# Where the first operands of the down product are loaded, in a forward and backward kernel on one core

## The chip, the cores and the metric

The kernel runs on one core of a Trainium2 chip. The metric is device time in microseconds (us), the median of several executions; lower is better. The core's engines that matter here are TensorE (PE, matrix products), VectorE (DVE, elementwise work), ScalarE (ACT, mostly copies out of PSUM), and the queues on which transfers (DMAs) are issued: SyncE's (SP), ScalarE's and GpSimd's (POOL). Each engine and each queue takes its instructions in the order in which the compiled program holds them.

## The reference

The reference is the vector-Jacobian product of one layer, with its forward output. Only these lines bear on the change:

```python
xn = _layernorm(x, axis=-1)                  # x: 2048 x 1024
s  = _A_ref(xn, A_k, A_v, ...)               # a long convolution, by Fourier transforms
g  = einsum("bsd,df->bsf", xn, w_gate)       # F = 3584
u  = einsum("bsd,df->bsf", xn, w_up)
h  = g * u
bm = einsum("bsf,fd->bsd", h, w_down)        # the down product
out = x + s * silu(bm)
# outputs: out and the gradients of all inputs and weights
```

## The kernel before, in words

All matrices are bf16 in 128-row blocks. The part around the change is the forward pass; it takes about the first 570 us of the span.

**The gate/up stage** (line 645) makes g and u. The weights come in 14 slabs of 256 columns of each matrix (`load_slab`, line 536, two transfers of 512 KB, two buffers `wslab`). A unit (`gu_unit`, line 629) takes one slab and four row blocks: 32 matmuls of 512 columns into `psg` (two PSUM buffers), four ACT casts to `gut` (line 647; two SBUF buffers in the last slabs), one store of `gut` to DRAM (`GUd`, line 654, on ACT's queue). The product h = g*u of a unit (`hN`, line 659, on DVE) is traced at the first row of the next unit. The turn of h (`turn`, line 669) comes a unit later still, after the second row of the unit after next: eight transposes on PE (line 674), one ACT copy to `hT` (line 675; two buffers from pool `fg` here), and the store of turned h to DRAM (`store`, line 664; `HTd`, 256 KB, on SP's queue through the helper `ld`, line 60).

**The convolution** runs beside it. Its DVE instructions are fixed in program order among those of the units (`pinned`, line 207, names most DVE lines as L213). `tick()` at the end of each row of a unit lets the generator `conv_forward` go on by an amount from its planned costs.

**The last two slabs**, 12 and 13, are done in eight units, line 951 on: slab 12 on row blocks 0-3 and 4-7, slab 13 on the same, then both again on row blocks 8-15. I number these units u0 to u7, and the units of slab 11 before them u-4 to u-1.

**The down product** (`bm_mm`, line 966, PSUM tiles `psbm`) starts behind u7. For its first two row blocks it reads turned h from `HT0` (two SBUF areas: `HT0[0]` holds h's blocks of 128 features 0 to 15, `HT0[1]` those from 16 on) and the down weight from `WD` (seven pieces of 512 rows, 1 MB each). `load_wd(j)` (line 937) and `ht_rows` (line 940) give their sources. Each of the first 28 feature blocks takes four matmuls: two row blocks by two halves of the output's columns. The areas of `WD` and `HT0` are eight old buffers, `U0` to `U7`, that were free at that point or come free as the last units stop reading their rows.

Program order is not the order in which a queue issues. The planner of the framework orders what is traced by its own estimates, unless something ties it: `tc.issue_after(x)` makes each traced instruction that is on x's engine or queue come behind x in that queue; it adds no semaphore. In the kernel before, line 947 ties `load_wd(0)`, `load_wd(1)` and the load of the whole of `HT0[0]` behind `slab_ld`, the last transfer of slab 13. The load of the first half of `HT0[1]` (line 963) is traced behind u1 and is tied to nothing.

Of the kernel before, what the change touches and what calls it, by code (L numbers as in the profile page):

```python
# [19 lines left out]
def build_kernel(  # L20
# [12 lines left out]
    P = 128  # L33
# [6 lines left out]
    SLW = 256  # L40
    NSL = F // SLW
# [18 lines left out]
    def ld(out, in_):  # L60
        return nc.sync.dma_start(out=out, in_=in_)
# [3 lines left out]
    def st(out, in_):  # L65
        ins = nc.gpsimd.dma_start(out=out, in_=in_)  # L66
        if PINQ[0]:
            tc.keep_in_program_order(ins)
        return ins

    def sta(out, in_):
        return nc.scalar.dma_start(out=out, in_=in_)
# [39 lines left out]
    HTd = [[dram.tile([n, S // 2], BF16, name=f"HTd{i}{n}") for n in (24 * P, 4 * P)] for i in range(2)]  # L112
# [99 lines left out]
    def tt(o, a, b, op):  # L212
        pinned(V.tensor_tensor(o, a, b, op))  # L213
# [35 lines left out]
    def fwd4_half(x, i, wp, psp, first=None):  # L249

        pe_us[0] += 1.75
        SP = wp.tile([P, 2, 2, 512], F32, name="SP", bufs=2)
        for par in range(2):
            ps = psp.tile([P, 2, 2, 256], F32, name="psF")
            cmm(ps[:, 0], T4[par], x, (i, i + 4), first if i == 0 else None, True)
            cmm(ps[:, 1], T4[par], x, (i + 2, i + 6))
            nc.scalar.copy(out=SP[:, :, par], in_=ps[:].rearrange("p s k x -> p s (k x)"))
        return SP

    def fwd4_buf(wp):  # L260
        return wp.tile([P, 2, 2, 4, 256], F32, name="W", tag="W")
# [244 lines left out]
    def u8(i, pat="p (a x) -> p a x", **kw):  # L506
        return U[i][:].rearrange(pat, **kw)
# [94 lines left out]
    def turn_late():  # L602
        for i, (x, q, qi) in enumerate(turn_rows):
            ps = ps_st.tile([P, DC, P], BF16, name="tr")
            for dc in range(DC):
                tr_ln[0] = nc.tensor.transpose(ps[:, dc, :], x[:, dc * P:(dc + 1) * P], ident[:])
            act_copy[0] = nc.scalar.copy(out=XNT[q][:, :, qi * P:(qi + 1) * P], in_=ps[:])
        turn_rows.clear()
# [6 lines left out]
    def defer(fn):  # L615
        later.append([0, fn])

    def flush(age=0):

        for e in later:  # L620
            e[0] += 1
        while later and later[0][0] >= age:
            later.pop(0)[1]()
# [5 lines left out]
    def gu_unit(sl, b0, n, w, tick):  # L629

        if n == 4:
            turn_of[0] += 1
            if turn_of[0] % 3 == 0 and sl < NSL - 2:
                gut = U[5][:, 2048:4096].rearrange("p (a i f) -> p a i f", a=2, i=4)
            else:
                gut = fg.tile([P, 2, 4, SLW], BF16, name="gut")
            hN = fg.tile([P, 2, 4, P], BF16, name="hN", bufs=3)
        else:
            gut = lnp.tile([P, 2, 2, SLW], BF16, name="gut_s", bufs=6)
            hN = lnp.tile([P, 2, 2, P], BF16, name="hN_s", bufs=6)  # L640
        for i in range(n):
            q, qi = divmod(b0 + i, 4)
            ps = ps_gu.tile([P, 512], F32, name="psg")
            for dc in range(DC):
                gu_mm[0] = nc.tensor.matmul(ps[:], XNT[q][:, dc, qi * P:(qi + 1) * P],  # L645
                                            w[:, dc].rearrange("p a f -> p (a f)"), start=(dc == 0), stop=(dc == DC - 1))
            nc.scalar.copy(out=gut[:, :, i], in_=ps[:].rearrange("p (a f) -> p a f", a=2))  # L647
            flush(5)
            if i == 0:
                turn_late()  # L650
            hn[0]()
            hn[0] = nop
            tick()
        sta(GUd[sl, b0 // 8][:, :, b0 % 8:b0 % 8 + n], gut[:, :, 0:n])

        def multiply():
            with tc.issue_after(last.ins) if b0 + n <= 4 and chunk[0] <= 2 else nullcontext():
                by_half = lambda t: t.rearrange("p i (a f) -> p a i f", a=2)
                tt(hN[:, :, 0:n], by_half(gut[:, 0, 0:n]), by_half(gut[:, 1, 0:n]), MUL)
            st(Hd[sl][:, :, b0:b0 + n, :], hN[:, :, 0:n])  # L660
            defer(turn)
        hn[0] = multiply

        def store(hT):
            fr, so = sl % 12 * SLW, b0 % 8 * P
            ld(HTd[b0 // 8][sl // 12][fr:fr + SLW, so:so + n * P].rearrange("(a f) s -> f a s", f=P),
               hT[:, :, 0:n].rearrange("f a i s -> f a (i s)"))

        def turn():
            hT = fg.tile([P, 2, 4, P], BF16, name="hT") if chunk[0] > 5 else lnp.tile([P, 2, 4, P], BF16, name="hT_s", bufs=5)  # L670
            ps = ps_tr.tile([P, 2, 4, P], BF16, name="tr")
            for a in range(2):
                for i in range(n):
                    nc.tensor.transpose(ps[:, a, i, :], hN[:, a, i, :], ident[:])  # L674
            nc.scalar.copy(out=hT[:, :, 0:n], in_=ps[:, :, 0:n])
            store(hT)

    h_out = []
    EIGHT = ((0, 0), (0, 1), (7, 0), (7, 1))
    INV8 = (2, 4, 5, 6, 7)  # L680
    SHIFT_W = 8 * 2.3
# [3 lines left out]
    def conv_forward():  # L685
# [78 lines left out]
        def half(ds, x, i, first=None):  # L764
            if (ds, int(first is not None)) not in EIGHT:
                return fwd4_half(x, i, cf, ps_cv, first)
            SP = cf.tile([P, 2, 2, 512], F32, name="SP", bufs=2)
            fwd8_half(x, i, SP, ps_cv, first, True)
            return SP

        def transform(ds, kind, sp, X, C, ahead, step):

            if ds == 7 and kind == 1:
                S_["forward"] = False
            if (ds, kind) in EIGHT:
                W = fwd4_buf(cs)[:].rearrange("p a b c x -> p (a b c) x")
# [29 lines left out]
        for ds in range(8):  # L806
# [9 lines left out]
            own_room = lambda X: X[:].rearrange("p a x -> p (a x)").bitcast(F32).rearrange("p (a x) -> p a x", a=8)[:, 0:4]  # L816
            eight = (ds, 1) in EIGHT
            if ds == 0:
# [40 lines left out]
    F_TOTAL = 4 * SHIFT_W + 3.0 + 8 * (0.5 + FWD4_W + 1.3 + PROD_W + INV_W) + 10.0 - 0.95 * 8 * (4 * 1.75 + 0.95 + 4 * 0.9)  # L859
    F_TOTAL += len(EIGHT) * (FWD8_W - 9.6 + 0.95 * 1.75) - 2.0  # L860
    F_TOTAL += len(INV8) * (INV8_W - INV_W + 0.95 * 1.8)
# [56 lines left out]
    def tick(by=1):  # L918
        cnt[0] += by
        if cnt[0] == -4:  # L920
            pump((SHIFT_W + 4.05) / F_TOTAL)
        if cnt[0] >= -2:
            pump((SHIFT_W + (F_TOTAL - SHIFT_W) * (cnt[0] + 6.5) / (NT + 3.5)) / F_TOTAL)
# [13 lines left out]
    def load_wd(j):  # L937
        return ld(WD[j], B_w_down[j * 512:(j + 1) * 512, :].rearrange("(c p) d -> p c d", p=P))

    def ht_rows(bp, f0, f1):  # L940
        j = (bp % 4) * 256
        return HTd[bp // 4][f0 // 24][f0 % 24 * P:(f0 % 24 + f1 - f0) * P, j:j + 256].rearrange("(c f) s -> f c s", f=P)
# [3 lines left out]
    HT0 = [u8(4, a=16), u8(5, a=16)]  # L946
    with tc.issue_after(slab_ld.ins):
        load_wd(0)
        load_wd(1)
        ld(HT0[0], ht_rows(0, 0, 16))  # L950
    for hf in range(2):
        if hf == 1:
            load_wd(2)
        for sl in range(NSL - 2, NSL):
            for b0 in (8 * hf, 8 * hf + 4):
                gu_unit(sl, b0, 4, slabs[sl - NSL + 2], tick)
            if (hf, sl) == (1, NSL - 2):
                wd_ld = load_wd(3)
                ld(HT0[1][:, 8:12], ht_rows(0, 24, 28))
            if (hf, sl) == (0, NSL - 2):  # L960

                assert len(h_out) == 8
                ld(HT0[1][:, 0:8], ht_rows(0, 16, 24))
    hn[0]()

    def bm_mm(ps, ht, i, fc):
# [606 lines left out]
def kernel(  # L1573
# [22 lines left out]
    out_9: bass.AP,  # L1596
):
    build_kernel(
        ctx, tc,
        A_q, A_k, A_v, A_shift_k, A_ssm_k, A_ssm_D, B_x, B_w_gate, B_w_up, B_w_down, grad_out,  # L1600
# [32 lines left out]
```

## Time and profile before

| what | value |
|---|---|
| median of three runs | 1928.96 us (1928.41 to 1929.06) |
| the profiled execution, its own time | 1929.12 us |
| its span in the profile | 1927.3 us |
| PE busy in the span | 1910.5 us (99%) |
| DVE busy | 1554.9 us (81%) |
| ACT busy | 638.9 us (33%) |
| units u0 to u7 on PE | about 448.0 to 518.3 us |
| first matmul of the down product | 518.27 us |
| SP queue, loads in question: `HT0[1]` first half, 512 KB | issued 445.85 us |
| slab 13, two of 512 KB | issued 448.22 and 448.65 us |
| `WD[0]`, `WD[1]`, 1 MB each | issued 451.43 and 452.96 us |
| `HT0[0]`, 1 MB | issued 456.75 us |

All times in the text are us from the start of the span. A row of a timeline has the start, the time taken, the engine, the line of the kernel, the operation, output and input tiles, the count that was merged into it, and in brackets the idle time of the engine ahead of it and what ended it. The rows of an engine named SPq or ACTq are transfers being issued; the time taken is that of the issue, and the landing comes later. Buffer numbers are left out: `U<-HTd` is a load of turned h into one of the `U` areas. A row of the table of windows has the stretch, its length, the busy time (and instruction count) of PE, PEld (weight loads), DVE, ACT and POOL, the clock granted to PE as a share of full speed, the busy share of the transfer engines, and GB/s.

### The profile page before, as it was taken

The numbers are of one execution on the slowest core, as the hardware profiler recorded it, in microseconds if no ns is written. First come the engines' busy times: TensorE is split into PE (matmuls) and PEld (weight loads), VectorE is DVE, ScalarE is ACT, GpSimd is POOL, SyncE is SP. The second block draws the span as 40 slices with busy tenths as digits, with TensorE's granted clock in tenths as the row PEclk, the third lists the DMA queues.
The fourth block names the chain that finished last, engine by engine and source line by source line (L and its number), as shares of the span: only waits on it lengthen the run. The fifth ranks groups of instructions, "written<-read, shape, count | busy, mean of one in ns | idle before, by whom it ended". The sixth has DMA issues, their size and how long they took to land.

```text
span 1927.3 us, 27409 instructions
## 1 busy us (share of the span) xinstructions
PE 1910.5 (99%) x10946; PEld 1027.7 (53%) x10946; DVE 1554.9 (81%) x1715; ACT 638.9 (33%) x943; POOL 330.1 (17%) x461
## 2 busy tenths in 40 slices
PE   8999999999999999999999999999999999999999
PEld 5555655554544456665666666664444444444444
DVE  8999999999967555888899999999996403387884
ACT  5754655545422233342222322222222102011113
POOL 5121212201112211000122131021111101011111
PEclk9999999999999999999999999999999999999999
DMA  8786867768789988656778788575797999899884
GB/s 291 270 261 217 260 208 236 222 216 270 253 267 318 307 291 254 210 200 222 261 242 263 236 247 262 202 266 182 225 253 175 140 213 219 162 183 183 196 183 157
DMA packets 451359, 444.41 MB, mean 231 GB/s; under 512 B 268800, under 2 KB 371612, under 8 KB 436768
## 3 DMA queue, kind: packets, MB, share of 16 engines
q1 hardware_dynamic: 394848, 243.36, 47.8%
q0 software_dynamic: 40064, 169.95, 27.8%
q10 hardware_dynamic: 16320, 29.36, 4.2%
q8 instruction: 85, 1.39, 0.3%
q14 instruction: 42, 0.34, 0.1%
HBM read 194.00 MB, written 185.64 MB: 197 GB/s over the span
## 4 chain that ended last, share of the span: by engine, by line
PE 94%; DVE 2%; DMA 2%; ACT 1%; issue 0%; SPq 0%; ACTq 0%
PE psb L1341 20%; PE psx L1471 20%; PE psg L645 18%; PE psb L1324 10%; PE psb L1419 9%; PE psbm L968 9%; PE psF L235 3%; PE psY L438 1%; PE tr L674 1%; DMA HTd<-hT 1%; PE psY L1127 1%; PE psx L1419 1%; DVE W L213 1%; PE psY L449 1%; DVE bst L561 0%; DMA wslab<-in_B_w_gate_dram 0%
## 5 line engine op out<-in xcount | busy, mean ns | idle before, releaser
L645 PE MATMUL psg<-wslab,U 128*128 128x512 bf16 x1792 | 409.5, 380 | 7.3 <-ACT gut L647 4.6
L1341 PE MATMUL psb<-U,U 128*128 128x512 bf16 x1792 | 397.1, 379 | 0.0
L1471 PE MATMUL psx<-U,dgut 128*128 128x512 bf16 x1536 | 332.8, 379 | 0.0
L1471 PEld LDWEIGHTS <-dgut 128*128 128x128 bf16 x1792 | 175.3, 98 | 211.4
L1341 PEld LDWEIGHTS <-U 128*128 128x128 bf16 x1792 | 175.2, 98 | 198.0
L645 PEld LDWEIGHTS <-U 128*128 128x128 bf16 x1792 | 172.9, 98 | 193.4 <-issue 9.0
L1324 PE MATMUL psb<-wdt,U 128*128 128x256 bf16 x1792 | 205.6, 273 | 0.0
L1324 PEld LDWEIGHTS <-U 128*128 128x128 bf16 x1792 | 175.3, 98 | 29.2
L213 DVE TENSOR_TENSOR W<-W 128x1024 f32<-128x1024 f32 (+1 forms) x186 | 183.9, 1005 | 3.9
L1419 PE MATMUL psb<-U,U 128*128 128x512 bf16 x816 | 177.1, 379 | 0.0
L1346 ACT CAST wb<-psb 128x512 bf16<-128x512 f32 x112 | 65.6, 586 | 315.4 <-PE psb L1341 310.5
L968 PE MATMUL psbm<-U,ht 128*128 128x512 bf16 x672 | 145.7, 379 | 0.0
L1419 PEld LDWEIGHTS <-U 128*128 128x128 bf16 x896 | 87.5, 98 | 104.5
L647 ACT CAST gut<-psg 128x512 bf16<-128x512 f32 x156 | 91.5, 588 | 124.1 <-PE psg L645 120.0
L1503 ACT ACTIVATE dx_t<-dxn 128x1024 bf16<-128x1024 f32 x15 | 15.9, 1057 | 321.8 <-DVE dxn L213 317.9
L968 PEld LDWEIGHTS <-ht 128*128 128x128 bf16 x672 | 65.6, 98 | 78.6
L1179 DVE SCALAR_TENSOR_TENSOR dkp<-dkT,kT 128x1024 bf16<-128x1024 bf16 (+2 forms) x64 | 78.4, 1224 | 35.3 <-DMA dkT<-DKSHd 33.6
L213 DVE TENSOR_TENSOR U<-U,dht 128x2048 bf16<-128x2048 bf16 x56 | 68.3, 1221 | 46.7 <-ACT dht L1326 46.6
L1326 ACT CAST dht<-psb 128x512 bf16<-128x512 f32 x112 | 65.7, 587 | 116.3 <-PE psb L1324 116.3
L66 POOL DMA_DIRECT2D Hd<-hN x54 | 37.0, 686 | 283.2 <-DVE hN L213 280.8
L213 DVE TENSOR_TENSOR dxn<-psx,dxna_t 128x1024 f32<-128x1024 f32 x15 | 18.3, 1222 | 79.1 <-PE psx L1471 74.5
L1450 ACT CAST wbs<-psb 128x512 bf16<-128x512 f32 x51 | 29.9, 586 | 145.9 <-PE psb L1419 134.0
(237 smaller groups left out, 2445.5 us busy)
## 6 DMA issues: line engine op xcount, KB each, us to landing
U<-GUd SPq DMA_DIRECT2D x28, 1024.0 KB, 7.2
DGd<-U SPq DMA_DIRECT2D x28, 1024.0 KB, 5.9
GUd<-gut ACTq DMA_DIRECT2D x39, 512.0 KB, 6.3
out_dram<-wb SPq DMA_DIRECT2D x112, 128.0 KB, 4.2
U<-Hd SPq DMA_DIRECT2D x14, 1024.0 KB, 6.0
Hd<-hN POOLq DMA_DIRECT2D x54, 256.0 KB, 4.2
HTd<-hT SPq DMA_DIRECT2D x52, 256.0 KB, 3.6
ht<-HTd SPq DMA_DIRECT2D x6, 1536.0 KB, 11.0
```

Of the source, the lines that this page charges most:

```text
L213: pinned(V.tensor_tensor(o, a, b, op))
L235: mm = nc.tensor.matmul(ps[:, k].rearrange("p (c d) -> p c d", c=2), T[:, r, k, :], xr[:, r], start=(n == 0), stop=(n == len(rs) - 1 and ( ...
L645: gu_mm[0] = nc.tensor.matmul(ps[:], XNT[q][:, dc, qi * P:(qi + 1) * P], w[:, dc].rearrange("p a f -> p (a f)"), start=(dc == 0), stop=(dc ...
L647: nc.scalar.copy(out=gut[:, :, i], in_=ps[:].rearrange("p (a f) -> p a f", a=2))
L968: mm = nc.tensor.matmul(ps[:, dh * 512:(dh + 1) * 512], ht(fc)[:, i * P:(i + 1) * P], WD[fc // 4][:, fc % 4, dh * 512:(dh + 1) * 512], sta ...
L1179: ins = V.scalar_tensor_tensor(prod[:].rearrange("p r d -> p (r d)")[:, lo:H], dkT[:, 0, lo:H], 1.0, kT[:, 0, 13 + m + lo:13 + m + H], op0 ...
L1324: nc.tensor.matmul(ps[:, x * SLW:(x + 1) * SLW], DBMT[2 * hf + g][:, dc, (b % 4) * P:(b % 4 + 1) * P], wdt[:, dc, :], start=(dc == 0), sto ...
L1326: nc.scalar.copy(out=dht[:, 2 * e:2 * e + 2].rearrange("p b f -> p (b f)"), in_=ps[:])
L1341: nc.tensor.matmul(ps[:], XN[b // 4][:, b % 4, dc * P:(dc + 1) * P], dgus[b // 8][:, :, b % 8], start=(b == 0), stop=(b == NB - 1))
L1346: nc.scalar.copy(out=wb[:, dc % 2].rearrange("p a f -> p (a f)"), in_=ps[:])
L1419: nc.tensor.matmul(ps, h[:, f, b, :], DBM[b // 4][:, b % 4, dh * 512:(dh + 1) * 512], start=(b == 0), stop=(b == NB - 1))
L1471: nc.tensor.matmul(ps[:, dh * 512:(dh + 1) * 512], t[n][:, f, i * P:(i + 1) * P], WGU[n][:, f, dh * 512:(dh + 1) * 512], start=(n == 0 and ...
```

## The change

`store` keeps the newest store of turned h. Only `load_wd(0)` stays tied to slab 13. Four other loads are traced one by one, behind the units u0 to u3, and each is tied behind the store of turned h that is newest at that point. The load of `HT0[0]` is split in two halves of 512 KB; the load of the first half of `HT0[1]`, until now untied and traced behind u1, is the fourth.

```diff
         def store(hT):
             fr, so = sl % 12 * SLW, b0 % 8 * P
-            ld(HTd[b0 // 8][sl // 12][fr:fr + SLW, so:so + n * P].rearrange("(a f) s -> f a s", f=P),
+            ht_st[0] = ld(HTd[b0 // 8][sl // 12][fr:fr + SLW, so:so + n * P].rearrange("(a f) s -> f a s", f=P),
                hT[:, :, 0:n].rearrange("f a i s -> f a (i s)"))
...
+    ht_st = [None]
...
     HT0 = [u8(4, a=16), u8(5, a=16)]
     with tc.issue_after(slab_ld.ins):
         load_wd(0)
-        load_wd(1)
-        ld(HT0[0], ht_rows(0, 0, 16))
+    early = [lambda: load_wd(1), lambda: ld(HT0[0][:, 0:8], ht_rows(0, 0, 8)),
+             lambda: ld(HT0[0][:, 8:16], ht_rows(0, 8, 16)), lambda: ld(HT0[1][:, 0:8], ht_rows(0, 16, 24))]
     for hf in range(2):
         if hf == 1:
             load_wd(2)
         for sl in range(NSL - 2, NSL):
             for b0 in (8 * hf, 8 * hf + 4):
                 gu_unit(sl, b0, 4, slabs[sl - NSL + 2], tick)
+                if early:
+                    with tc.issue_after(ht_st[0].ins):
+                        early.pop(0)()
             if (hf, sl) == (1, NSL - 2):
                 wd_ld = load_wd(3)
                 ld(HT0[1][:, 8:12], ht_rows(0, 24, 28))
-            if (hf, sl) == (0, NSL - 2):
-
-                assert len(h_out) == 8
-                ld(HT0[1][:, 0:8], ht_rows(0, 16, 24))
+    assert len(h_out) == 8 and not early
```

## The prediction, made before the changed kernel was run

> **What bounds the kernel now.** The page first: PE is busy 1910.5 of 1927.3 us, so all that a change of order can win is in PE's 16.8 us of other time. Next the list of waits of PE: its longest in mid-kernel is 3.28 us, a psg matmul that waits for an ACT cast of gut. I looked for it in the timelines of PE, ACT, DVE and SP between 440 and 560 us, beginning with PE:
>
> ```profile
> 471.04 1.89 PE L645 MATMUL psg<-wslab,U 128*128 128x512 bf16 x8
> 476.21 5.30 PE L645 MATMUL psg<-wslab,U 128*128 128x512 bf16 x16 [3.28 <-ACT gut L647]
> 514.82 3.62 PE L645 MATMUL psg<-wslab,U 128*128 128x512 bf16 x16
> 545.89 0.27 PE L438 MATMUL psY<-HX,TI 128*128 128x256 bf16 x1 [1.34 <-DVE HX L283]
> 551.11 20.23 PE L968 MATMUL psbm<-U,U 128*128 128x512 bf16 x93
> ```
>
> PE stops between u2 and u3 for 3.28 us, and the 16 matmuls behind the gap take 5.30 us where 16 others take 3.62. The table of windows has the reason, the granted clock (third number from the end), 0.57 here and 1.00 in the stretches before and behind:
>
> ```profile
> 472.00:476.00 4.00, 0.93 (x5) 0.29 (x4) 2.69 (x3) 1.34 (x2) 0.00 (x0) 1.00 0.47 163
> 476.00:480.00 4.00, 3.79 (x10) 1.37 (x10) 1.48 (x3) 2.69 (x5) 0.50 (x1) 0.57 0.83 236
> 480.00:484.00 4.00, 4.00 (x27) 2.06 (x25) 3.93 (x6) 2.15 (x4) 0.19 (x1) 1.00 0.74 291
> ```
>
> ACT and DVE show what stops PE and who else stops:
>
> ```profile
> 474.66 1.01 ACT L675 COPY hT<-tr 128x1024 bf16<-128x1024 bf16 x1 [5.88 <-DMA HTd<-hT]
> 475.57 0.59 ACT L647 CAST gut<-psg 128x512 bf16<-128x512 f32 x1
> 472.27 2.48 DVE L213 TENSOR_TENSOR W<-W 128x1024 f32<-128x1024 f32 x2
> 478.52 0.69 DVE L213 TENSOR_TENSOR hN<-gut 128x1024 bf16<-128x1024 bf16 x1 [3.76 <-ACT gut L647]
> 502.62 0.69 DVE L213 TENSOR_TENSOR hN<-gut 128x1024 bf16<-128x1024 bf16 x1 [0.33 <-ACT gut L647]
> 519.09 0.69 DVE L213 TENSOR_TENSOR hN<-gut 128x1024 bf16<-128x1024 bf16 x1 [0.52 <-ACT gut L647]
> 545.15 2.50 DVE L283 SCALAR_TENSOR_TENSOR HX<-W 128x512 bf16<-128x512 f32 x4
> ```
>
> ACT's copy to hT of u0 waits 5.88 us for a buffer: the store of the hT two units older (u-2) has not landed. Behind that copy on ACT stands the gut cast that frees PSUM for PE and gives DVE its hN. The SP queue, and the chain of waits (start, duration, what), say why the store was late:
>
> ```profile
> 451.43 5.16 SPq L61 DMA_DIRECT2D U<-in_B_w_down_dram  x2
> 456.75 0.39 SPq L61 DMA_DIRECT2D U<-HTd  x1
> 457.24 11.46 SPq L61 DMA_DIRECT2D HTd<-hT  x1
> ...
> 457.24 17.34 DMA HTd<-hT
> ```
>
> The copy for that store ended at 453.19, but the store was issued at 457.24, behind slab 13, WD[0], WD[1] and HT0[0], took 11.46 us to issue, and landed 17.34 us later, at 474.58; ACT went on at 474.66. The other hT stores of this stretch land in 2.1 to 6.5 us.
>
> From 519 to 547 us the chain of waits runs on DVE (m, KX, W, HX), not on PE: the last HX of the convolution ends at 547.65 and PE waits 1.34 us for it. From 551 us on PE runs without a wait into the next stages, so whatever PE has won there is won at the end.
>
> **The change part by part.**
>
> *The late store.* Behind slab 13 only WD[0] stays ahead of the store of u-2; WD[1] (u-2), the halves of HT0[0] (u-1, u0) and HT0[1]'s first half (u1) each come behind the store named. The last one also leaves its place at 445.85, ahead of slab 13. SP moved 5.0 MB from 445.85 to the landing of the store of u-1 at 475.3 (HT0[1] 0.5, slab 1, WD 2, HT0[0] 1, two stores 0.5): 0.17 MB/us. From 448.22, slab 13, WD[0] and the store are 2.25 MB: an estimate of 13.2 us at that rate, landing at 461.5. The other end: WD[0] landed 14.9 us after its issue at 451.43, at 466.3; the store right behind it, with 2.1 to 6.5 us of its own, 468.4 to 472.8. The copy wants the buffer at about 468.7 (transposes at 467.99 for 0.61). PE idled 3.28 of the 5.88 us and DVE 3.76, so the copy may come 2.1 us late, at 470.8, before DVE feels it. I take the estimate, as it is worked out from what stands in the queue, and no wait. For the next two buffers the same rate gives: store of u-1 behind WD[1], 468.8, wanted about 477; store of u0 about 473, wanted about 484.
>
> *What PE and DVE get.* PE: 3.28 of idle and 5.30 - 3.62 = 1.68 of slow clock, 4.96. DVE: the 3.76. Of hN's two later waits, 0.33 and 0.52, PE's lead over DVE (4.96 - 3.76 = 1.20) covers both, 0.85. So DVE's chain is 4.61 earlier, and PE comes to psY 4.96 earlier: its wait there grows from 1.34 to 1.34 + 4.96 - 4.61 = 1.69. **The end moves by DVE's 4.61**, with 3.76 (the later waits stay) and 4.96 (PE alone) as its bounds.
>
> *The longer wait at psY* could cost clock. Behind 1.34 us of idle the clock stayed 1.00, behind 3.28 it fell; 1.69 is nearer to the first: I take nothing, and 1.68 is the price if not. The Trainium skill, "TensorE: Matmul & The Clock Gate", section "HAM oscillation — how this bites in real kernels", warns of gaps over some 3.4 us, and the 3.28 us here already fell to it, so its limit is a little high. By that rule the new gap is free and the sum stays; by a drop it would be 2.9.
>
> *PE's other gap*, 0.77 us at 460.22, comes from the store of gut at 448.85 on ACT's queue (10.6 us to land). SP still has slab 13 and WD[0] to move then, so I leave the gap. DVE has no idle time there, so its loss or gain, 0 to 0.77, is absorbed at psY. Against a gain here speaks the Trainium skill too, "DMA: Bandwidth & Descriptors", section "Queues, rings and completion order": the transfer engines take turns between queues packet by packet, so a shorter line in SP's queue alone does not speed ACT's. By it the term is 0; by the row, between 0 and 0.77, the sum is the same.
>
> *The moved loads.* One more issue on SP, 0.36 to 0.39 us, beside nothing that waits. Each load now waits for its store, thus for ACT's hT copy; behind it in SP's queue stand WD[2], WD[3] and later stores. Needed by PE, with the 4.96 taken off: HT0[0] first half 513.3, WD[1] about 517, HT0[0] second half 521.4, HT0[1] 528.2 (feature block 16 is 43 matmuls of 0.216 us behind 523.88). Issued, estimated: 462, 454, 470 and 478; with the longest landing seen in the stretch, 17.2 us, they are there by 496 at worst. That is 25 us or more of cover; without it PE would wait one for one. WD[2] (476.15) and WD[3] (485.44) keep 30 us. POOL's and ACT's queues are passed by nothing. The 1.5 MB moved falls to 462-490, where the busy share of the transfer engines was 0.47 to 0.88 from 472 on.
>
> Sum: 1929.12 - 4.61 = 1924.5 for the profiled execution; it is 0.16 above the median, so **1924.4** against 1928.96, 0.24% less. A measurement of this kernel tells about 0.2% (3.9 us) from no change, so the forecast lies just on the faster side.
>
> **Rivals.**
>
> *PE gets all (0.09).* The planner, with other transfers to place, puts psY elsewhere or the 0.77 goes as well, and DVE no longer decides: 4.96 up to 3.28 + 1.68 + 0.77 + 1.34 = 7.07; 1921.9 to 1924.0. For: all four gaps are PE's. Against: DVE's chain is unbroken from 478 to 547, and the psY matmuls are the last link of it.
>
> *Only part of the stall goes (0.22).* The store of u-2 lands past 470.8 (the end of 472.8 would cost 2.0), or the clock falls at psY (1.68), or the planner shifts a few psF or psY matmuls among the units: gain 0 to 3.8, 1925.2 to 1929.0. For: 1 MB of slab and 1 MB of WD are still ahead of that store, and slow transfers with short packets are what filled the queue. Against: 3 us or more of room by the rate.
>
> *The change does nothing (0.04).* The planner might have placed the loads so anyway, or DVE is held by another wait: 1929.0. Against: the order of before is in the SP rows.
>
> *The wait comes back at the next buffers (0.13), slower.* One mechanism: each later store of turned h now has a fresh load of 0.5 or 1 MB directly ahead of it in SP's queue. If such a store again needs 17 us, as the one at 457.24 did, the hT copies of u1 and u2 wait; it decides from a landing past 477 + 2.1 for the store of u-1, or 484 + 2.1 for that of u0. Price as now, 3.76 on DVE to 4.96 on PE for each: two new stalls for one removed, -4.61 + 7.5 to 9.9, +2.9 to +5.3: 1931.9 to 1934.3. For: the 1 MB loads of this stretch took 14.9 to 17.2 us to land. Against: the queue is shorter by 1.5 MB at 457, and 8 us of room.
>
> **How the numbers follow.** Forecast (gain 3.8 to 4.96) 0.52, the rest as above. Faster by over 0.2% is the forecast but for its lowest end, 0.50, and PE gets all, 0.09: 0.59. Within 0.2%: the part, the null and that end, 0.27. Slower: the return 0.13 and 0.01 from the part: 0.14. The range: half of the best rival is cut off below, 1922.9, and the slower one above 1929.5: about 0.17 outside. The forecast's own range is 1924.0 to 1925.2.
>
> **What would show it.** Right: no ACT wait on HTd<-hT near 470; the store of u-2 issued near 453.3 and landed before 470; no psg gap between u2 and u3; granted clock 1.00 from 476 to 480; hN without its 3.76; the wait before psY near 1.7 us, some 4.6 us earlier, and psbm unbroken behind it. Wrong: a new wait on HTd<-hT at a later unit, a psbm matmul waiting for a load of U, a clock below 1.00 behind psY, or another order of DVE's or PE's rows.

## The result, and the profile after

| | before | after |
|---|---|---|
| median of 22 runs each, us | 1929.41 | 1925.61 |
| lowest to highest | 1928.02 to 1943.39 | 1923.53 to 1930.68 |
| ratio after / before | | 0.9972, 95% interval 0.9961 to 0.9984 |
| profiled execution | 1929.12 | 1923.68 |
| its span | 1927.3 | 1921.9 |

The kernel is faster, by 0.28% by the ratio (5.4 us of 1929.1), by 3.8 us between the medians. The ratio is close to that of the means (1926.25 and 1931.58), and eight times of the kernel before, from 1931.2 to 1943.4, lift its mean; the medians give the more careful size. The two profiled executions differ by 5.44 us; that this is the ratio's 5.4 is chance. Two marks that both timelines of PE have tell where: the transposes of u-2 (451.48 before, 451.04 after) and the first psbm matmul that reads an `ht` tile (571.18 and 565.81). The stretch between them, "the stretch" from here on, took 119.70 us and takes 114.77: **4.93 us**. The first psbm matmul behind it, before and after:

```profile
571.18 29.09 PE L968 MATMUL psbm<-U,ht 128*128 128x512 bf16 x134
565.81 34.48 PE L969 MATMUL psbm<-U,ht 128*128 128x512 bf16 x159
```

Another 0.44 us lies ahead of the stretch. It is there already at 406 us, where the programs are alike, and two more profiles of the changed program have the first mark at 450.90 and 450.68, so it is chance. Behind the stretch the two differ by 0.03 us (1356.12 and 1356.09 to the end of the span).

The changed program differs from the one before in SP's queue alone, by its order and by one load that is now two; in the traces up to 570 us the other engines hold the same instructions in the same order. The SP queue after:

```profile
449.09 0.82 SPq L61 DMA_DIRECT2D U<-in_B_w_down_dram  x1
452.77 0.37 SPq L61 DMA_DIRECT2D HTd<-hT  x1
453.19 1.13 SPq L61 DMA_DIRECT2D U<-in_B_w_down_dram  x1
460.12 0.37 SPq L61 DMA_DIRECT2D HTd<-hT  x1
460.59 0.55 SPq L61 DMA_DIRECT2D U<-HTd  x1
```

The store of u-2 is issued as soon as its copy is done and in 0.37 us, not 11.46. It lands 11.4 us later, at 464.2, not 474.6. ACT, the windows, DVE and PE after:

```profile
467.31 1.02 ACT L675 COPY hT<-tr 128x1024 bf16<-128x1024 bf16 x1
```

```profile
472.00:476.00 4.00, 4.00 (x26) 2.07 (x25) 3.97 (x5) 1.72 (x4) 0.69 (x1) 1.00 0.81 212
476.00:480.00 4.00, 4.00 (x20) 1.81 (x19) 3.93 (x7) 1.73 (x3) 0.00 (x0) 1.00 0.98 352
```

```profile
474.20 0.68 DVE L213 TENSOR_TENSOR hN<-gut 128x1024 bf16<-128x1024 bf16 x1
497.87 0.68 DVE L213 TENSOR_TENSOR hN<-gut 128x1024 bf16<-128x1024 bf16 x1
513.73 0.69 DVE L213 TENSOR_TENSOR hN<-gut 128x1024 bf16<-128x1024 bf16 x1
539.78 2.50 DVE L283 SCALAR_TENSOR_TENSOR HX<-W 128x512 bf16<-128x512 f32 x4
```

```profile
458.84 3.62 PE L645 MATMUL psg<-wslab,U 128*128 128x512 bf16 x16
540.52 0.27 PE L438 MATMUL psY<-HX,TI 128*128 128x256 bf16 x1 [2.47 <-DVE HX L283]
545.74 20.24 PE L969 MATMUL psbm<-U,U 128*128 128x512 bf16 x93
```

No bracket is left on the copy to hT, none on the three hN; PE is busy in all of 472 to 480 at full clock. The last HX starts 5.37 us earlier on the page, 4.9 us after the 0.46 us that DVE was ahead already. PE has one wait left in the stretch, and it has grown from 1.34 to 2.47 us, before psY. The page's chain of waits is of no use for the comparison: after the change it follows POOL's stores of h through here and puts 17% of the span down to "issue". The brackets in the timelines had to do its work.

### The profile page after: what moved, and what is told of

Its sections match the earlier page's. It is cut to its first block, busy times and chain, and to the rows that moved or that the text cites. A ratio compares the mean times of both kernels' runs of the same rounds, so it can differ in the third digit from the quotient of the medians.

```text
span 1921.9 us, 27410 instructions
## 1 busy us (share of the span) xinstructions
PE 1909.1 (99%) x10946; PEld 1028.1 (53%) x10946; DVE 1554.5 (81%) x1715; ACT 638.8 (33%) x943; POOL 330.9 (17%) x461
## 4 chain that ended last, share of the span: by engine, by line
PE 71%; issue 17%; DVE 6%; POOL 3%; DMA 3%; ACT 1%; SPq 0%; POOLq 0%; DVEq 0%; ACTq 0%
PE psx L1472 20%; PE psb L1342 20%; PE psb L1420 9%; PE psb L1325 9%; PE psg L645 8%; PE psF L235 2%; DVE W L213 1%; DMA A<-DYd 1%; POOL Hd L66 1%; PE psY L1128 1%; PE psY L438 1%; PE psx L1420 1%; DVE HX L213 1%; DVE KX L213 1%; DMA yf_t<-YFd 1%
```

## The experiments

Times are the median of each kernel's runs, beside it the median of the kernel before on the same chip. "Gap at 460" is PE's wait for ACT's gut cast there, "gap at psY" the one before the first waiting psY matmul; the stretch is from the profile. Lines shift by a few where lines were added.

| kernel | median (before) | ratio, interval | stretch | gap at 460 | gap at psY |
|---|---|---|---|---|---|
| before | | | 119.70 | 0.77 | 1.34 |
| after | | | 114.77 | 0 | 2.47 |
| again | 1925.06 (1928.30) | 0.9977, 0.9969 to 0.9986 | 116.39 | 0 | 2.63 |
| both_u0 | 1923.71 (1928.30) | 0.9976, 0.9966 to 0.9985 | 114.99 | 1.19 | 1.34 |
| ht1_late | 1925.03 (1928.30) | 0.9983, 0.9974 to 0.9991 | 116.18 | 0 | 1.38 |
| ht3 | 1923.89 (1928.30) | 0.9981, 0.9971 to 0.9990 | 114.78 | 0.80 | 1.52 |
| ht1_early | 1923.83 (1928.86) | 0.9977, 0.9967 to 0.9986 | 114.82 | 0.87 | 1.37 |
| pe_more | 1927.22 (1928.86) | 0.9996, 0.9987 to 1.0006 | 116.28 | 0 | 1.40 and 0.94 |
| before_later | 1927.88 (1928.86) | 0.9994, 0.9986 to 1.0003 | 117.38 | 1.26 | 0 |
| psy_later | 1927.47 (1928.86) | 0.9985, 0.9972 to 0.9998 | 111.99 | 0 | 0 |
| psy_again | 1921.98 (1928.50) | 0.9978, 0.9964 to 0.9992 | 111.96 | 0 | 0 |
| again2 | 1924.55 (1928.50) | 0.9982, 0.9974 to 0.9991 | 114.80 | 0 | 1.35 |

### again: the changed kernel once more

No edit.

> The changed kernel as it is, for one more profile and as the yardstick of the other runs. Queue theory (the order of SP's queue alone let the store of turned h of u-2 land in time, DVE then decides the end): 5.4 us less than before; no wait of ACT for the store, the matmul before psY waits about 2.5 us for HX. Clock side theory: of the 22 times of the changed kernel those with a mean granted clock of 1.000 lie at 1923.5 to 1924.4 and those with 0.999 above 1924.8; if the 2.5 us of PE's idle time before psY sometimes cost half the clock for 3.4 us, a profile with 0.999 shows the half clock right behind 540 us and the gap unchanged; if the slower times come from elsewhere, the stretch behind 540 stays at 1.00.

The gap was there, 2.63 us, and this time it cost clock. PE, then the windows (clock third from the end):

```profile
540.53 0.27 PE L438 MATMUL psY<-HX,TI 128*128 128x256 bf16 x1 [2.63 <-DVE HX L283]
541.90 1.91 PE L969 MATMUL psbm<-U,U 128*128 128x512 bf16 x4
```

```profile
540.00:544.00 4.00, 3.47 (x12) 1.50 (x12) 2.29 (x4) 0.59 (x1) 0.00 (x0) 0.67 0.47 113
544.00:548.00 4.00, 4.00 (x24) 2.30 (x22) 0.00 (x0) 1.75 (x4) 0.00 (x0) 0.90 0.00 0
```

Four psbm matmuls took 1.91 us, in the profile after 1.02. The clock lost 4 x (0.33 + 0.10) = 1.72 us, and the stretch is 1.62 us longer than after. The clock theory holds for this profile. The eleven times lie in two groups, 1923.1 to 1923.9 (four) and 1924.8 to 1925.8 (seven). The four have a mean clock of 1.000 over the whole run, the seven, the profiled one among them, 0.999; in the profiles one fall gives 0.999 (before, again, psy_later), and those without a fall have 1.000. So each run of the upper group seems to hold such a fall, but where it lies is seen in the profiled one alone. Over all runs of the changed kernel (here, in the result and in again2) 13 of 44 have 1.000. Of the four variants whose profiles show a gap of 1.3 to 1.5 us before psY (both_u0, ht1_late, ht3, ht1_early) 38 of 43 runs have it. That bears the theory out and does not prove it: pe_more, with a gap of 1.40 and another close behind, has 3 of 11, and psy_later, with no gap there, 4 of 12.

### both_u0: the store passes both loads, which stay together

```diff
     with tc.issue_after(slab_ld.ins):
         load_wd(0)
-        load_wd(1)
-        ld(HT0[0], ht_rows(0, 0, 16))
...
                 gu_unit(sl, b0, 4, slabs[sl - NSL + 2], tick)
+                if (hf, sl, b0) == (0, NSL - 2, 0):
+                    with tc.issue_after(ht_st[0].ins):
+                        load_wd(1)
+                        ld(HT0[0], ht_rows(0, 0, 16))
```

> The kernel before with one change: WD[1] and the whole of HT0[0] are tied behind the store of u-2, both at once behind u0; HT0[1]'s first half stays ahead of slab 13. Queue theory: the store of u-2 is issued near 453 and lands at 464 to 467, so the copy of u0 does not wait; the store of u-1 has 5 MB of the stretch ahead of it and itself, lands near 475 and is wanted near 476.5, so at most 1 us of wait: 4.5 to 5.4 us less than before, like the whole change. Rival (the loads must be spread one by one): the 2 MB right ahead of the store of u-1 bring the wait back one buffer later, with about 3.8 us of DVE and 3.3 of PE: 0 to 1.5 us less than before.

The store of u-2 landed at 466.6 and that of u-1, with 2 MB ahead of it, at 475.1; no copy waited:

```profile
461.35 8.80 SPq L61 DMA_DIRECT2D HTd<-hT  x1
```

The store took 8.80 us to issue and 13.7 to land, and it cost nothing, since its buffer is wanted only near 476. PE waited 1.19 us at 460 and 1.34 before psY. The rival falls: spreading is not needed. It is enough that the one store whose buffer is next passes the two loads. By median this kernel is 1.35 us below again.

### ht1_late: only the first half of HT0[1] moves

```diff
-            if (hf, sl) == (0, NSL - 2):
-
-                assert len(h_out) == 8
-                ld(HT0[1][:, 0:8], ht_rows(0, 16, 24))
+            if (hf, sl) == (0, NSL - 1):
+                with tc.issue_after(ht_st[0].ins):
+                    ld(HT0[1][:, 0:8], ht_rows(0, 16, 24))
```

> The kernel before with one change: only the first half of HT0[1] is tied behind the store of u1 and so leaves its place ahead of slab 13; WD[1] and HT0[0] stay ahead of the store of u-2. Queue theory: 0.5 MB less in the queue at 0.17 MB/us lets the store of u-2 land 3 us earlier, near 471.6; the copy of u0 waits about 2.9 us instead of 5.9, DVE under 1 us, PE under 0.5 us and without a fall of the clock: 3.5 to 4.2 us less than before. Rival (what counts is that the store passes WD[1] and HT0[0]): the store still lands past 473, 0 to 1 us less than before.

```profile
472.23 1.01 ACT L675 COPY hT<-tr 128x1024 bf16<-128x1024 bf16 x1 [4.35 <-DMA HTd<-hT]
```

```profile
476.09 0.69 DVE L213 TENSOR_TENSOR hN<-gut 128x1024 bf16<-128x1024 bf16 x1 [1.34 <-ACT gut L647]
```

The store landed at 472.2 (471.6 expected). ACT waited 4.35 us and not 2.9, as the copy was wanted a microsecond earlier, PE having lost nothing at 460; DVE 1.34 (under 1 expected); PE 1.75 and 0.44 (under 0.5), at full clock. The stretch is 3.5 us shorter, the median 3.3 us lower, a little less than the 3.5 to 4.2 that were expected. This is the dose between nothing and all: 0.5 MB less ahead of the store takes 2.4 of 3.76 us off DVE's wait.

### ht3: the same late store, another buffer

```diff
-            hT = fg.tile([P, 2, 4, P], BF16, name="hT") if ...
+            hT = U[5][:, 3072:4096].rearrange("p (f i s) -> p f i s", f=2, i=4) if (sl, b0) == (NSL - 2, 0) else fg.tile([P, 2, 4, P], BF16, name="hT") if ...
```

> The kernel before with one change: turned h of u0 goes into a spare part of U5 in place of a buffer that the store of u-2 still holds; all loads stay where they were, SP's order too. Queue theory (the harm of the late store is the one buffer it holds): ACT's copy of u0 does not wait, PE's 3.28 us and DVE's 3.76 us are gone, clock 1.00 behind 476, while the store of u-2 still lands near 474: 4.5 to 5.4 us less than before. Rival (the crowded transfers themselves hold the stage, by the stores of gut or by the weight slab): the stall moves to another wait in the same stretch, 0 to 2 us less than before.

```profile
456.99 11.03 SPq L61 DMA_DIRECT2D HTd<-hT  x1
```

```profile
468.05 1.02 ACT L675 COPY U<-tr 128x1024 bf16<-128x1024 bf16 x1
```

The store is as late as before (17.0 us from issue to landing, at 474.0), and ACT does not wait. The stretch is 114.78 us, that of the whole change. None of the three hN waits, and the clock is 1.00 from 472 to 480. So the harm of the crowded queue that reached the end was the one buffer that the store held. PE still waited 0.80 us at 460 for the store of gut, and that did not reach the end. Its profiled execution lost 1.8 us much later to a load of `dgut`, with which the change has nothing to do.

### ht1_early: the changed kernel with HT0[1] back in front

```diff
-             lambda: ld(HT0[0][:, 8:16], ht_rows(0, 8, 16)), lambda: ld(HT0[1][:, 0:8], ht_rows(0, 16, 24))]
+             lambda: ld(HT0[0][:, 8:16], ht_rows(0, 8, 16))]
...
+            if (hf, sl) == (0, NSL - 2):
+                ld(HT0[1][:, 0:8], ht_rows(0, 16, 24))
```

> The changed kernel with one part undone: the first half of HT0[1] goes back to its place ahead of slab 13, untied; WD[1] and the two halves of HT0[0] stay one by one behind the stores. It asks what took away PE's wait of 0.77 us at 460 us for the store of gut, and whether that matters. Queue theory: with the 0.5 MB of short packets back ahead of slab 13 the store of gut issued near 448 lands past 458 again, PE waits 0.7 to 1.2 us near 460; no wait for the store of turned h; the wait before psY is 1.3 to 1.7 us in place of 2.5, the clock there stays 1.00, and the best times are those of the changed kernel within 0.5 us, with a median 1 us lower. Rival (the 0.77 us were won by the end too): best times 0.7 us or more above the changed kernel's best.

```profile
459.74 3.61 PE L645 MATMUL psg<-wslab,U 128*128 128x512 bf16 x15 [0.87 <-ACT gut L647]
540.43 0.27 PE L438 MATMUL psY<-HX,TI 128*128 128x256 bf16 x1 [1.37 <-DVE HX L283]
```

The store of gut issued near 448 lands after 10.7 us (after: 7.1), PE waits 0.87 us at 460 again, the gap at psY shrinks by 1.10, and the stretch is 114.82. What PE loses at 460 it does not lose at psY: DVE's HX decides. Ten of its twelve times lie between 1923.49 and 1924.14, beside 1923.1 to 1923.5 for the best times of the changed kernel; the median is 5.0 us under that of the kernel before on the same chip; on two other chips the changed kernel gained 3.2 and 4.0.

### pe_more: more work for PE

```diff
+    more = ps_gu.tile([P, 512], F32, name="psg")
+    for n in range(8):
+        nc.tensor.matmul(more[:], HT0[0][:, 0, 0:P], WD[0][:, 0, 0:512], start=(n == 0), stop=(n == 7))
```

> The changed kernel with eight more matmuls of 512 columns (1.73 us of PE) ahead of the down product, into a PSUM tile that nobody reads. The planner also moves three psbm matmuls (0.65 us) from before the first waiting psY to behind it. DVE theory: HX ends as before, the wait before psY shrinks to 2.5 - 1.73 + 0.65 = 1.4 us, the end moves by those 0.65 us alone, and with a gap of 1.4 us the clock does not fall: best times 0.6 us above the changed kernel's best, its median below or within 0.5 us of the changed kernel's median in spite of the added work. PE theory (DVE's chain is no bound): 1.7 us more than the changed kernel throughout.

```profile
540.67 0.27 PE L438 MATMUL psY<-HX,TI 128*128 128x256 bf16 x1 [1.40 <-DVE HX L283]
541.87 0.27 PE L438 MATMUL psY<-HX,TI 128*128 128x256 bf16 x1 [0.94 <-DVE HX L283]
```

The time decides nothing, and my expectation was wrong: idle time stayed at 2.34 us, and the stretch grew by 1.5 us, which is close to the 1.7 of the PE theory. The traces say what grew. In the changed kernel three psbm matmuls stand ahead of the first of these psY matmuls and four between the two (rows of the profile after):

```profile
537.24 0.81 PE L969 MATMUL psbm<-U,U 128*128 128x512 bf16 x3
540.63 1.02 PE L969 MATMUL psbm<-U,U 128*128 128x512 bf16 x4
```

In pe_more the planner has moved all seven, not the expected three, behind both waits; at 0.216 us each they are the 1.5 us. Both psY matmuls start as late behind the first mark as in the changed kernel (89.49 and 90.69 us, against 89.48 and 90.69), with 1.73 us more work of PE ahead of them. So up to there it is HX that sets the time, and behind it PE's work that is left.

### before_later, psy_later and psy_again: PE's gap filled

```diff
     bm_first(range(fc_, NF))
+    ps2 = ps_bx.tile([P, D], F32, name="psbm")
+    for fc in range(10):
+        bm_mm(ps2, ht1[0], 0, fc)
     drain()
...
+            ps = ps2 if (bp, i) == (1, 0) else (ps_bx if (2 * bp + i) % 3 == 2 else ps_bm).tile([P, D], F32, name="psbm")
+            for fc in range(10 if (bp, i) == (1, 0) else 0, NF):
```

> The changed kernel with one more edit: ten feature blocks of the down product's third row block (20 matmuls, 4.3 us) are traced ahead of the convolution's last pieces, so the planner places them before psY; nothing is left out. DVE theory (what the change left on the path is DVE's last HX, for which PE stands 2.5 to 2.6 us before psY, and that gap sometimes costs half the clock for 3.4 us): the wait before psY is gone, HX still ends near 542.3, the granted clock is 1.00 behind it in every run, so 2.5 us less than the best times of the changed kernel (1921.0 to 1921.5) and about 3.5 to 4 less than its median, and a narrower spread. Rival (PE's work or a later stage sets the end, the gap is filled only to be paid later, by the third row block's PSUM or the gates): a new wait of PE behind 545 us, 0 to 1 us less than the changed kernel.

> The kernel before with the edit of psy_later alone: 20 matmuls of the third row block ahead of the convolution's last pieces, all loads as they were. DVE theory: PE's wait of 1.34 us before psY goes, the stall at 472 to 476 and its half clock stay: 1.3 us less than before, no more. With psy_later it gives what the loads are worth when DVE no longer decides: the difference of the two should be all that PE lost at 460 and 472 us, 0.77 + 3.28 + 1.68 = 5.7 us. Rival (the psY matmuls were late only because of the stall): no change from before.

> psy_later once more, beside the changed kernel on the same chip. Its first times fell into two groups, four at 1920.5 to 1921.6 and eight at 1925 to 1933, and its profile had lost 3.2 us ahead of 450 us, where its program is the changed kernel's, and 2.2 us behind 560 us in two waits for loads. DVE theory: the stretch from u0 to the fifth row block of the down product (451.04 to 565.81 us in the changed kernel, 114.8 us) takes 112.0 us again with the clock at 1.00 behind psY; if the loss ahead of 450 was chance, the median lies 2.5 to 4 us under the changed kernel's. Rival (the 2.5 us are given back behind 560 us): the waits for loads of turned h and of dy are there again, with 1.5 us or more, and the median is no lower than the changed kernel's.

PE in psy_again runs through:

```profile
534.73 6.64 PE L969 MATMUL psbm<-U,U 128*128 128x512 bf16 x30
541.20 0.66 PE L438 MATMUL psY<-HX,TI 128*128 128x256 bf16 x4
```

The stretch is 111.99 and 111.96 us in the two profiles, 2.8 less than after. With the same edit the kernel before needs 117.38; the difference, 5.4 us, is what the loads are worth where PE decides. That it is near the 5.7 expected is luck: the expected sum has 1.68 us of slow clock, which this profile lacks, and the idle time that was to make up the rest was longer, 1.26, 3.30 and 0.44 us. before_later gained 2.3 us of stretch in its profile and not 1.3, mainly because this time the stall of 3.30 us did not cost clock:

```profile
476.46 1.89 PE L645 MATMUL psg<-wslab,U 128*128 128x512 bf16 x8 [3.30 <-ACT gut L647]
```

```profile
476.00:480.00 4.00, 3.10 (x14) 1.35 (x14) 1.23 (x3) 3.32 (x5) 0.25 (x1) 1.00 0.73 210
```

As a whole kernel psy_later is not settled. On the second chip it is 2.6 us below the changed kernel (1921.98 against again2's 1924.55; eight of twelve times between 1920.6 and 1922.2); on the first, eight of twelve lay above 1925, and the ratios to the kernel before, 0.9978 and 0.9985, do not part it from the changed kernel. The first profile of psy_later had lost 3.2 us ahead of the stretch, at the start of the kernel. There PE waited for the first weight slab and then ran at half clock, and the nine matmuls took 3.78 us; in psy_again the same nine took 2.10 behind a wait of 1.69.

```profile
16.76 3.78 PE L645 MATMUL psg<-wslab,U 128*128 128x512 bf16 x9 [3.14 <-DMA wslab<-in_B_w_gate_dram]
```

Behind the stretch stood two waits for loads that the changed kernel's profiles do not have, 0.61 us at 615 and this one:

```profile
746.91 1.03 PE L235 MATMUL psF<-A,TF 128*128 128x256 bf16 x8 [1.55 <-DMA A<-DYd]
```

The second profile has neither wait and ends at 1919.2, the shortest span here. That accounts for the one profiled run. Of the other long ones it is known that all seven on the first chip have a mean clock of 0.999 or less; where they lose it stays open, and so does whether the edit has a part in the new waits. The expectation of a clock of 1.00 in every run, and of a narrower spread, was wrong.

### again2: a third profile of the changed kernel

> The changed kernel once more as the yardstick of psy_again, and for a third look at the gap of 2.5 us before psY. If the clock falls by chance behind that gap, the times again form two groups some 1.5 us apart (near 1923.5 and near 1925), and the profile belongs to the upper one just when its clock behind 540 us is half. If the slower times come from the start of the kernel, the profile's clock behind 540 us is 1.00 whatever its time.

The clock stayed 1.00 and the time, 1923.31, is in the lower group, as the clock theory wants; but the gap was 1.35 us only, so it is no test of the clock behind a gap of 2.5. PE had lost 0.43 and 0.32 us near 486, behind a store of gut that landed after 10.8 us, so the gap before psY differs between runs of one kernel. The stretch, 114.80, is that of after although PE came to psY later: once more DVE's end decides.

## Why the prediction was right

**The late store**: right, place and size. The issue was forecast near 453.3 and was 452.77; the landing 461.5 with ends to 472.8, and was 464.2, 2.7 us late of the estimate and 3.1 ahead of the copy that wanted the buffer. The stores of u-1 and u0 were put at 468.8 and about 473 and landed at 468.3 and 472.3. The rate of 0.17 MB/us in SP's queue, from the profile before, was good enough to order what would be late; both_u0 and ht1_late came within 1 us of it as well. That the one buffer is all of the harm that reaches the end is shown by ht3.

**DVE's 4.61**: right in kind, 0.3 too small. It came to 4.9: 3.85 at the first hN, 0.43 and 0.61 at the later two (differences of start times between the rows shown), against 3.76, 0.33 and 0.52. The idle time in brackets leaves out about 0.1 us a wait by which back-to-back instructions overlap. The sum should go by start times.

**PE's lead covers the two later waits, and DVE's end sets the stage's end**: right. ht1_early, both_u0 and ht3 lost 0.8 to 1.2 us of PE at 460 and kept the stretch within 0.25 us.

**The wait at psY**: forecast 1.69, measured 2.47. The term that failed is PE's gap at 460, which I left at 0.77: it went, since the store of gut lands after 7.1 us instead of 10.6. ht1_early shows the cause, the 0.5 MB of HT0[1] ahead of slab 13: that store took 10.6 to 11.1 us in the five profiles that have this load there, 6.8 to 9.4 in the seven that have not. That 2.47 - 1.69 is just about 0.77 is partly luck, as DVE gained 0.3 more than forecast. The rest is again the brackets: PE's rows overlap by 0.17 us where nothing waits (534.73 + 6.64 and 541.20 in psy_again), so the two gaps were worth 0.94 and 3.45, and 1.34 + 0.94 + 3.45 + 1.68 - 4.9 = 2.5. The reason I took from the Trainium skill's rule that the engines take turns, that the length of SP's line does not matter to ACT's queue, is my own step from it, and it was wrong here; the sum was not touched, as PE's gain was absorbed at psY. That the 0.77 went as well was a condition of the rival "PE gets all"; it came true, and DVE still set the end.

**The clock behind psY**: "I take nothing, and 1.68 is the price if not." Both happen. With the gap at 2.47 the clock stayed, at 2.63 in again it fell and cost 1.6 us. It belongs into the forecast as a chance and not as a choice. Between the medians on one chip the gain is 3.2 us (again) and 4.0 us (again2), less than the 5.4 between the profiles. The mean clocks fit: in again the medians of the runs with 1.000 and with 0.999 are 1.6 us apart, the price of one fall. That the half clock behind psY makes all of this difference was not shown. So the rival "only part of the stall goes" was partly true, through this one of its mechanisms.

**The moved loads** cost nothing: no psbm matmul waited for a load of U. **The wait comes back** did not happen, not even in both_u0, built to provoke it.

Of the 5.44 us between the two profiles, 0.44 are chance ahead of the stretch. The forecast of 1924.4 lay 1.2 us under the median of 22 runs and 0.7 above the profiled execution. The median, 1925.61, lies 0.4 us above the forecast's own range of 1924.0 to 1925.2, and the gain between the medians, 3.8 us, at the low end of its 3.8 to 4.96; the forecast had started from 1928.96, and over 22 runs the kernel before has 1929.41. Two errors, the 0.3 us of DVE too little and the clock left out, pull in opposite ways.

## What to carry to other kernels

A store is late by what stands ahead of it in its own queue, and it harms by the buffer it holds: list the bytes ahead of it, divide by the rate the queue shows, and compare with the time when its buffer is next wanted. Let just that store pass the loads (or give it another buffer); the rest need not be spread. When a stall that held two engines goes, the gain is that of the engine that ends last, and the other's gain turns into a longer wait, which here sometimes costs clock. both_u0 shows the odd side of it: PE loses 1.19 us earlier, waits 1.34 before psY and not 2.5, all its runs keep a clock of 1.000, and its median is 1.35 us below the changed kernel's. Filling that wait with work that is ready is the next step; it took 2.8 us off the stretch, and what it does for the whole kernel is not settled.

## What the runs showed of the hardware

**The clock falls behind short gaps, and not always.** Of the gaps of PE in mid-kernel, those of 1.3 to 1.8 us never cost clock in a profile, 2.47 did not and 2.63 did, 3.28 did and 3.30 did not; at the start of psy_later one of 3.14 did. A fall lasts some 3.4 us at half clock (1.72 us lost in again). It does not begin at one time after the gap: PE went on at 540.53 in again and at 476.21 before, and windows of half a microsecond put the fall at 541.4 (clock 1.00, then 0.86, then 0.50 from 541.5 on) and at 476.3. The Trainium skill, "TensorE: Matmul & The Clock Gate", section "What's actually happening", says that the activity window is free-running, so that its phase differs from run to run; gaps of one length with and without a fall would fit that, but no run here shows the window. Its section "HAM oscillation — how this bites in real kernels" puts the limit at gaps of over about 3.4 us; the 2.63 us in again do not agree with that as a safe bound.

**One queue had nearly all of four microseconds.** In the kernel before, while ACT's store of gut (issued at 448.85, landed after 10.6 us) and POOL's store of HFd (449.37, 9.6 us) were under way, SP's queue (q1; packets, MB, share of the engines' time) had nearly all of 450 to 454 us with its packets of some 500 B:

```profile
q1 hardware_dynamic: 2052, 1.03, 94.9%
q10 hardware_dynamic: 94, 0.19, 13.9%
q0 software_dynamic: 13, 0.01, 1.3%
```

q10 is ACT's queue. The Trainium skill, "DMA: Bandwidth & Descriptors", section "Queues, rings and completion order", has the engines take turns between queues packet by packet; with 2052 packets against 94 and 13 no such turn shows in these four microseconds. How many packets of the other two queues were ready in that time, the profile does not show, nor whether its packets are those of the rule, so it is a doubt about the rule's use and no proof against it.
